# Another order of the same steps for a recurrence followed by a feed-forward block, with two filler matmuls fewer

## The chip, the cores and the metric

The kernel runs on one core of one Trainium2 chip. The metric is the device time of one execution in microseconds (us), given as the median of several executions. A run is called slow when it is more than 1.5% above the fastest of the same kernel; slow runs are left out of ratios. Engines are named as the profile names them: PE (tensor engine), PEld (its weight loads), DVE (vector), ACT (scalar), POOL (GpSimd), SP (the sync engine, which here only issues transfers).

## The reference

Two stages follow each other. The first is a linear recurrence over 768 time steps for 4 batches and 8 heads of 48 channels; the second is a feed-forward block over the resulting 3072 rows.

```python
for t in range(S):
    cur = np.einsum('bhd,bhe->bhde', u[None] * kt, vt)
    y[:, :, t] = np.einsum('bhd,bhde->bhe', rt, state + cur)
    state = wt[:, :, :, None] * state + np.einsum('bhd,bhe->bhde', kt, vt)
...
h = x @ w_in                       # 3072 x 384  @  384 x 2048
g = 0.5 * h * (1.0 + np.tanh(c * (h + 0.044715 * h * h * h)))
return g @ w_out                   # 3072 x 2048 @ 2048 x 384
```

## The kernel before

The work is cut into 12 units of 256 rows (three stretches of time by four batches). For each unit the recurrence is computed in chunks (scores `mt`, masked into `sc`, products `y`, a state `p`), its rows are transposed, and they go through the two matrix products `mm1` (line 626) and `mm2` (line 652). The order of everything is one list of words. A word is a step, its unit and part, a letter for the engine where there is a choice (A, D, P or S), and after `@` the bank of PE's accumulation memory that it takes.

```python
ORDER = """
const.3.D load.w.0.0 const.2.D load_u.A clr.sc.2.P clr.lwl.0.D load.w.0.1 clr.rq.1.P lnL.0.0
... (101 more lines) ...
"""
for word in ORDER.split():
    ... # load ACT's table set if this word needs another one
    step(word)
```

Each engine is given its instructions in the order of the list, and in the traces of both kernels they start in it, by kind of step: in each trace all 607 instructions of ACT, DVE, POOL and SP that I could match to words, and of PE's matmuls 2,278 of 2,280 before and 2,274 of 2,278 after the change; the few others are score products that start up to 0.04 us ahead of the last ones of a state product. So a word that waits holds up what stands behind it on its engine. The steps that the argument touches:

```python
def warm(i, e):                        # i filler matmuls ("dummies"), results never read
    t = bank([P, 512], FP, f"dummy{i}")
    for _ in range(i):
        PE.matmul(t[:, 0:256], warm_src[:, 0:P], warm_src, start=True, stop=True)

def sel(q, e):                         # the diagonal term of a unit, on PE
    ... PE.matmul(st["y", q][c2], diag[...], st["vsc", q][...], ...)

def p(q, e):                           # a unit's addition to the state, on PE
    ... PE.matmul(p2[c2][:, g, :], kt[rows, g, t2, :, :], vt[rows, t2, ds(2 * g, 2), :], **flags)

def mm1(q, i, e):                      # 6 matmuls of 256 columns
    ... PE.matmul(h[:, f, :], w_t, xt[:, :, cb, :], ...)

def ob(q, c2, e): ...                  # copy of a result, on ACT or DVE
def store(q, c2, e):                   # one or two transfers, issued by ACT or by SP
    ... (ACT if e == "A" else SP).dma_start(out=out[ds(row + i, n), cols], in_=t[ds(i, n)])
```

A dummy is a weight load and a matmul in PE's stream of instructions (the trace has 50 of each). The list has 50 of them, all before the first `mm1`. They are there to keep PE busy in the start-up; run u3 below shows what happens to PE's clock without 34 of them.

Of the kernel before, what the change touches and what calls it, by code (L numbers as in the profile page):

```python
# [29 lines left out]
const.3.D load.w.0.0 const.2.D load_u.A clr.sc.2.P clr.lwl.0.D load.w.0.1 clr.rq.1.P lnL.0.0  # L30
clr.sc.0.D const.0 clr.S.0.D clr.kk.2.D clr.lwl.1.P clr.rq.0.P load.w.1 clr.sc.1.P lnL.0.1
warm.16@0 cm.0@0 const.1.P clr.S.1.D lnL.1 ep.0@1 load.k.0 warm.1@2 cx.0@2 clr.kk.1.D
const.4.P ub@3 load.r.0 uc.A cz.0@4 clr.kk.0.D em.0 ez.0 clr.sc.3.D cz.1@5 cx.1@6 ex.0
const.6.A load.r.1 kk.0.0 kk.0.1 load.k.1 rq.0.0 rq.0.1 cm.1@7 ex.1 rq.1.0 warm.2@3 T.0.0@3
ep.1@0 rq.1.1 em.1 rka.0.P warm.3@2 T.0.1@2 load_win.1 load.v.0 warm.4@1 T.1.1@1 Tc.0.0.D
ez.1 clr.lw.2.D load.v.1 kk.1.0 rkb.0.P kk.1.1 Tc.0.1.A load.w.2 Tc.1.1.A load.k.2 al.1
mt.0.1@60 vb.0.A load_win.0 dg.0 rka.1.P mk.0.1.0 load.r.2 al.0 mt.0.0@32 warm.4@7 T.1.0@7
rkb.1.P Tc.1.0.A vb.1.A load.v.2 mk.0.0.0 warm.5@1 p.0@15 mk.0.1.1 mk.0.0.1 warm.4@4
mt.1.0@46 load_win.3 load.w.3 vsc.0 warm.7@3 y.0.0@37 load.k.3 sm.0.0 mk.1.0.0 mt.1.1@02
dg.1 y.0.1 vsc.1 ww.2.P const.5.A warm.4@1 p.1@14 load_win.2 sel.0 mk.1.1.0 a5.0.1 mk.1.0.1  # L40
mk.1.1.1 y.1.0@06 xs.0.0.D sm.1.0 y.1.1 X.0.0@2 clr.rq.2.P xs.0.1.A ln.2 sa.0.1 kw.2.P X.0.1
cum.2@7 Xc.0.A sel.1 a5.1.1 xd.2@1 clr.lw.1.P xs.1.0.A ez.2 xs.1.1.A mm1.0.3@3 sm.0.1
load.w.4 mm1.0.0@2 load.r.3 load.k.4 al.2 ex.2 X.1.0@0 rka.2.P X.1.1 kk.2.0 mm1.0.2@5
mm1.0.1@6 kk.2.1 load_wout.0 rw.2.P Xc.1.D T.2.0@7 mm1.1.2@0 gl.0.2 mm1.0.7@5 gl.0.3
clr.S.3.D rq.2.0 Tc.2.0.A gl.1.2 mm1.1.7@3 sa.1.1 rq.2.1 mm1.1.3@7 gl.0.0 rkb.2.P clr.S.2.D
mm1.0.6@0 clr.lw.0.P gl.0.1 T.2.1@1 sm.1.1 gl.1.3 dg.2 gl.1.7 load_wout.1 mm1.1.6@2 load.r.4
gl.1.6 load.v.4 Tc.2.1.D mm1.1.1@6 gl.0.6 dI.2.1 mm1.0.5@7 mt.2.1@43 dI.2.0 mt.2.0@21 gl.0.7
vb.2.A mk.2.1.0 gl.1.1 mk.2.0.0 mm1.0.4@0 gl.0.4 gl.0.5 load.k.6 mm1.1.0@5 ww.3.P mk.2.0.1
mm1.1.5@4 rka.3.P load.v.3 kw.3.P mk.2.1.1 load.k.5 gl.1.5 mm1.1.4@6 gl.1.0 y.2.0@20 load.w.5
gl.1.4 p.2@17 ww.4.P y.2.1 mm2.0.1.0@3 mm2.1.1.0@4 ln.3 mm2.0.0.0@5 rw.3.P mm2.1.1.1  # L50
mm2.1.1.2 mm2.0.1.1 mm2.0.0.1 mm2.0.0.2 sm.2.0 load.v.5 xs.2.0.D cum.3@6 rkb.3.P mm2.0.1.2
mm2.1.1.3 mm2.1.0.0@1 mm2.0.1.3 mm2.0.0.3 mm2.1.0.1 a5.2.1 xs.2.1.D X.2.0@2 mm2.1.0.2 xd.3@0
mm2.0.0.4 mm2.1.1.4 mm2.0.0.5 mm2.1.1.5 sa.2.1 mm2.1.1.6 mm2.0.0.6 sm.2.1 load.w.6 mm2.1.0.3
mm2.0.1.4 ex.3 mm2.0.1.5 al.3 mm2.1.1.7 ez.3 kk.3.0 mm2.1.0.4 ln.4 rq.3.0 X.2.1 Xc.2.A kw.4.P
kk.3.1 rw.4.P rq.3.1 mm2.1.0.5 load.r.7 mm2.0.1.6 cum.4@7 mm2.0.1.7 xd.4@0 dg.3 ob.1.1.A
load.r.5 ob.0.1.A T.3.1@6 ez.4 mm2.0.0.7 rka.4.P mm2.1.0.6 mm1.2.0@2 Tc.3.1.D ex.4
store.0.1.S ob.0.0.D T.3.0@4 rq.4.0 mm2.1.0.7 mm1.2.1@3 Tc.3.0.D dI.3.0 dI.3.1 al.4 mm1.2.4@6
mm1.2.3@5 gl.2.0 ob.1.0.A gl.2.1 store.0.0.S store.1.1.S gl.2.4 rkb.4.P rq.4.1 kk.4.0
mt.3.1@24 kk.4.1 vb.3.A load.k.7 load.r.6 mt.3.0@10 mk.3.0.0 store.1.0.S mm1.2.6@3 gl.2.3
mm1.2.2@6 mm1.2.5@7 mk.3.0.1 mk.3.1.0 vb.4.A mm2.2.1.0@1 mm2.2.1.1 p.3@50 gl.2.2 ww.5.P  # L60
rka.5.P gl.2.6 kw.6.P y.3.0@26 kw.5.P mk.3.1.1 gl.2.5 y.3.1 p.4@34 sm.3.0 dg.4 mm2.2.1.2 ln.5
sa.3.1 sa.4.0 mm2.2.1.3 mm2.2.0.0@7 a5.3.1 xs.3.0.A mm1.2.7@5 mm2.2.1.4 dI.4.1 sm.3.1 sm.4.0
mm2.2.0.1 mm2.2.0.2 X.3.0@2 mm2.2.1.5 xs.3.1.A sa.4.1 X.3.1 ww.6.P vb.5.P T.4.0@6 mm2.2.0.3
mm2.2.0.4 rw.5.P cum.5@0 mm2.2.1.6 mm2.2.0.5 xd.5@3 gl.2.7 load.w.7 Tc.4.0.D mm2.2.1.7 Xc.3.A
T.4.1@5 al.5 mm1.3.7@2 ex.5 mm2.2.0.6 ez.5 sm.4.1 mm2.2.0.7 rq.5.0 mm1.3.4@6 ln.6 Tc.4.1.D
gl.3.7 rq.5.1 mm1.3.1@4 ob.2.0.D kk.5.0 rkb.5.P mm1.3.0@5 mm1.3.3@3 kk.5.1 mt.4.0@27 ob.2.1.A
dI.4.0 mt.4.1@10 gl.3.1 dg.5 mm1.3.5@4 gl.3.0 mm2.3.0.0@5 gl.3.4 load.w.8 mk.4.1.0 rw.6.P
load.k.8 gl.3.5 mm1.3.6@6 mk.4.0.0 mm1.3.2@1 gl.3.3 mk.4.1.1 mk.4.0.1 dI.5.0 mm2.3.0.1 gl.3.6
ww.7.P cum.6@2 xd.6@7 p.5@43 y.4.0@06 gl.3.2 y.4.1 load.v.6 mm2.3.0.2 mm2.3.0.3 ez.6 sa.5.0
a5.4.1 Td.5.1 kw.7.P mm2.3.0.4 mm2.3.1.0@1 sm.5.0 ln.7 ex.6 store.2.0.S load.w.9 mm2.3.1.1  # L70
ww.8.P kk.6.0 mm2.3.0.5 xs.4.1.A dI.5.1 a5.4.0 sa.5.1 rw.7.P mm2.3.1.2 T.5.0@4 rka.6.P kk.6.1
mm2.3.0.6 cum.7@6 xs.4.0.A X.4.0@0 load.r.8 mm2.3.0.7 rq.6.0 mm2.3.1.3 rq.6.1 X.4.1 mm2.3.1.4
mm2.3.1.5 rka.7.P Tc.5.0.A al.6 sm.5.1 load.w.10 ob.3.0.A rkb.6.P mt.5.1@74 mt.5.0@23
mm2.3.1.6 xd.7@5 mk.5.1.0 mm2.3.1.7 Xc.4.A mk.5.0.0 al.7 mk.5.0.1 ez.7 mm1.4.0@0 vb.6.P ex.7
Td.6.0 ob.3.1.D mk.5.1.1 mm1.4.4@7 ln.8 mm1.4.6@2 gl.4.0 rkb.7.P kk.7.0 mm1.4.1@3 mm1.4.3@1
mm1.4.7@0 kk.7.1 gl.4.6 gl.4.1 gl.4.3 y.5.0@42 rq.7.0 p.6@63 y.5.1 a5.5.1 rq.7.1 kw.8.P dg.6
load.v.7 sa.6.0 sm.6.0 sa.6.1 mm2.4.1.0@5 mm1.4.2@1 mm2.4.1.1 a5.5.0 gl.4.7 mm1.4.5@0 gl.4.2
mm2.4.0.0@6 cum.8@1 dI.6.0 ww.10.P gl.4.4 mm2.4.1.2 xs.5.1.A Td.6.1 mm2.4.0.1 mm2.4.0.2
mt.6.1@72 dI.6.1 xs.5.0.D sm.6.1 gl.4.5 store.2.1.S vb.7.A ln.10 xd.8@3 mt.6.0@40 load.v.8
mk.6.1.0 mm2.4.1.3 mm2.4.1.4 al.8 mm2.4.1.5 mk.6.1.1 mk.6.0.0 rw.8.P Td.7.0 rka.8.P ez.8  # L80
mk.6.0.1 ww.9.P ex.8 mm2.4.1.6 X.5.0@7 mm2.4.1.7 X.5.1 mm2.4.0.3 kk.8.0 mm2.4.0.4 load.k.10
ob.4.1.A Xc.5.A dg.7 rq.8.0 rq.8.1 mm2.4.0.5 kk.8.1 load.k.9 p.7@24 sa.7.0 y.6.0@05 sm.7.0
dI.7.0 y.6.1 Td.7.1 dI.7.1 kw.9.P a5.6.0 mm2.4.0.6 xs.6.0.A mm2.4.0.7 mm1.5.0@7 mm1.5.2@3
mm1.5.5@0 load.r.10 ln.9 a5.6.1 Xd.6.0 gl.5.0 gl.5.5 vb.8.P xs.6.1.D gl.5.2 mm1.5.1@1
ob.4.0.D gl.5.1 rkb.8.P mm1.5.3@2 mm1.5.7@7 gl.5.3 sa.7.1 mm1.5.6@0 mt.7.0@53 gl.5.7
mt.7.1@61 p.8@2 rka.9.P sm.7.1 load.r.9 rw.9.P gl.5.6 load.v.9 mm1.5.4@7 mm2.5.1.0@4 cum.10@0
mk.7.0.0 cum.9@5 mk.7.0.1 gl.5.4 mm2.5.1.1 mm2.5.1.2 mk.7.1.0 xd.10@3 mk.7.1.1 Td.8.1 al.9
mm2.5.0.0@7 mm2.5.0.1 mm2.5.1.3 Xd.6.1 rkb.9.P y.7.0@61 y.7.1 mm2.5.0.2 sa.8.0 store.3.1.S
mm2.5.0.3 ex.10 sm.8.0 store.3.0.S mm2.5.1.4 xd.9@2 ex.9 a5.7.0 mm2.5.0.4 Td.8.0 xs.7.0.A
load.w.11 dg.8 mm2.5.1.5 mm2.5.1.6 rq.10.0 rw.10.P rq.9.0 kw.10.P Xd.7.0 a5.7.1 al.10  # L90
rka.10.P rq.9.1 mm2.5.1.7 vb.9.P dI.8.0 ez.9 rq.10.1 store.4.0.A ez.10 mm2.5.0.5 kk.10.0
mm2.5.0.6 ob.5.1.D ww.11.P load.k.11 mm1.6.0@6 dI.8.1 mm1.6.7@2 mm2.5.0.7 gl.6.0 Td.9.1
kk.9.0 mm1.6.4@3 ob.5.0.A kk.10.1 mm1.6.1@4 gl.6.7 xs.7.1.A mm1.6.2@6 Xd.7.1 kk.9.1 gl.6.1
gl.6.4 mt.8.1@07 mt.8.0@52 dg.9 kw.11.P mk.8.0.0 mk.8.0.1 dI.9.0 load.r.11 gl.6.2 p.9@1
mm1.6.3@4 rkb.10.P mm1.6.6@3 mk.8.1.0 mm2.6.0.0@6 mm2.6.0.1 gl.6.3 mk.8.1.1 Td.9.0
mm2.6.1.0@5 sa.9.0 dI.9.1 ln.11 mm2.6.0.2 rw.11.P mm2.6.1.1 mm2.6.1.2 gl.6.6 mm1.6.5@2
y.8.0@40 gl.6.5 y.8.1 sm.9.0 a5.8.0 mm2.6.0.3 mm2.6.1.3 a5.8.1 xs.8.0.D cum.11@7 mm2.6.0.4
xd.11@1 mm2.6.0.5 mm2.6.0.6 al.11 ez.11 mm2.6.1.4 kk.11.0 mm2.6.0.7 ob.6.0.D mm1.7.0@3 ex.11
mm1.7.3@2 Xd.8.0 xs.8.1.D mm1.7.4@4 kk.11.1 mm1.7.1@6 mm2.6.1.5 gl.7.3 gl.7.0 mm1.7.2@0
gl.7.4 mm2.6.1.6 dg.10 rq.11.0 gl.7.1 rka.11.P mt.9.1@72 mt.9.0@34 mm1.7.7@6 gl.7.2 mm1.7.5@0  # L100
mm2.6.1.7 mk.9.1.0 Td.10.0 mk.9.1.1 mm1.7.6@7 mk.9.0.0 store.4.1.S mm2.7.0.0@2 mk.9.0.1
mm2.7.0.1 load.v.10 gl.7.5 rkb.11.P mm2.7.0.2 y.9.0@30 y.9.1 a5.9.0 mm2.7.1.0@4 a5.9.1
mm2.7.0.3 gl.7.6 mm2.7.1.1 mm2.7.1.2 mm2.7.1.3 mm2.7.0.4 vb.10.P dI.10.0 xs.9.0.A Td.10.1
Xd.8.1 mm2.7.1.4 rq.11.1 mm2.7.0.5 Xd.9.0 gl.7.7 mt.10.1@17 dI.10.1 mt.10.0@36 xs.9.1.D
ob.6.1.D p.10@0 mk.10.0.0 mm2.7.0.6 store.5.1.S load.v.11 mk.10.1.0 mm2.7.1.5 mm2.7.0.7
# [639 lines left out]
```

## Time and profile before

| | |
|---|---|
| time, median | 180.57 us (180.31 to 181.15, 4 executions beside the changed kernel) |
| span of the profiled execution | 178.9 us |
| first `mm1` matmul starts | 23.91 us |
| last PE matmul starts | 175.71 us |
| from there to the end of the span | 3.17 us |
| PE idle after the first `mm1`, summed | 8.04 us by my count below |

The three rows of the middle split the span in a ramp, a middle and a tail, and the rest of this text compares kernels by these three numbers. The sum of idle time is the excess of each PE start-to-start distance over the median distance of the same kind of instruction in this kernel, with shorter distances counted against it. It is good for comparing, not as an absolute: between two kernels with the same PE instructions after the first `mm1`, it differs by just as much as the length of that stretch.

### The profile page before, as it was taken

Reading aid. Unit: us, or ns where it says so; the run is one execution under the profiler, and the core shown is the slowest. Engines: PE = TensorE matmul, PEld = TensorE weight load, DVE = VectorE, ACT = ScalarE, POOL = GpSimd, SP = SyncE. Lnnn points to the kernel's source line nnn. Section 1 sums busy time; section 2 is a strip of 40 time slices with the busy share of each in tenths; the row PEclk is TensorE's granted clock in tenths of the full one; section 3 lists DMA queues with packets and bytes.
Section 4 is the critical chain, followed back from the end, with each engine's and each line's share of the span. In section 5 each row is a group of like instructions: output and inputs, shape, how many; then the busy total and the mean of one; then the engine's idle time right before and its main releaser. Section 6 shows DMA issues by size and latency. Waiting matters only on the chain.

```text
span 178.9 us, 5496 instructions
## 1 busy us (share of the span) xinstructions
PE 172.0 (96%) x2280; PEld 135.7 (76%) x2280; DVE 114.6 (64%) x241; ACT 125.1 (70%) x215; POOL 109.9 (61%) x115
## 2 busy tenths in 40 slices
PE   7889889999999999999999999999999999999993
PEld 5456579966697788688689688687688787868772
DVE  7099979634888998989997998676291182200010
ACT  4595499872699998896988599996254644644831
POOL 7499998619998988998969986991514000000000
PEclk9999999999999999999999999999999999999999
DMA  5999999999999999999997879949297312510244
GB/s 136 261 268 238 255 236 266 219 234 234 270 265 221 317 284 171 276 150 239 177 208 173 174 189 206 154 78 199 54 222 84 89 48 66 117 41 0 44 90 134
DMA packets 74954, 31.68 MB, mean 177 GB/s; under 512 B 69681, under 2 KB 74418, under 8 KB 74930
## 3 DMA queue, kind: packets, MB, share of 16 engines
q1 hardware_dynamic: 71744, 26.91, 71.8%
q0 software_dynamic: 2144, 3.15, 9.9%
q10 hardware_dynamic: 1042, 1.28, 2.5%
q8 instruction: 18, 0.29, 0.7%
q14 instruction: 6, 0.05, 0.1%
HBM read 25.17 MB, written 4.72 MB: 167 GB/s over the span
## 4 chain that ended last, share of the span: by engine, by line
PE 79%; ACT 7%; DMA 6%; SPq 5%; POOL 1%; issue 0%
PE h L626 33%; PE o L652 33%; DMA w<-in_w_dram 6%; SPq L290 5%; PE mt L512 3%; ACT g L634 3%; PE y L534 2%; PE y L584 2%; PE T L433 2%; ACT L713 1%; ACT L711 1%; PE p L550 1%; PE Xp L601 1%; PE z L367 1%; ACT logw L328 1%; PE p L554 1%
## 5 line engine op out<-in xcount | busy, mean ns | idle before, releaser
L652 PE MATMUL o<-w_out_sb,g 128*128 128x384 bf16 (+1 forms) x400 | 73.3, 320 | 0.0
L626 PE MATMUL h<-xT,w_in_sb 128*128 128x256 bf16 x576 | 70.2, 273 | 0.2 <-ACT g L634 0.2
L626 PEld LDWEIGHTS <-w_in_sb 128*128 128x128 bf16 x576 | 62.2, 114 | 3.7
L652 PEld LDWEIGHTS <-g 128*128 128x128 bf16 x400 | 36.4, 98 | 16.5 <-ACT g L634 0.3
L634 ACT ACTIVATE g<-h 128x512 bf16<-128x512 f32 x48 | 32.9, 755 | 22.7 <-PE h L626 22.6
L519 DVE CAST_PREDICATED sc<-mask,mt 128x512 bf16<-128x512 uint16 x48 | 30.3, 684 | 10.5 <-PE mt L512 10.2
L638 ACT ACTIVATE g<-h 128x512 bf16<-128x512 f32 x48 | 26.1, 607 | 4.4 <-PE h L626 4.1
L456 POOL TENSOR_TENSOR rk<-k,u_bc 128x768 f32<-128x768 f32 x12 | 21.8, 1817 | 7.7 <-DMA k<-in_k_dram 5.1
L473 POOL TENSOR_TENSOR sc<-eye,dg 128x512 bf16<-128x512 bf16 x20 | 20.6, 1040 | 4.5 <-DVE dg L467 4.5
L462 POOL TENSOR_TENSOR rk<-rk,r 128x768 f32<-128x768 f32 x12 | 21.8, 1817 | 0.2
L272 DVE COPY ob<-o 128x384 f32<-128x384 f32 (+1 forms) x12 | 6.3, 534 | 21.4 <-PE o L652 21.4
L575 DVE TENSOR_TENSOR s<-p,al 64x192 bf16<-64x192 f32 x40 | 14.1, 353 | 2.5 <-PE p L550 1.7
L593 DVE CAST xs<-y 128x384 bf16<-128x384 f32 x12 | 6.7, 555 | 14.0 <-PE y L584 13.9
L711 ACT ACT_TABLE_LOAD x9 | 11.5, 1283 | 1.4 <-PEq L728 1.3
L567 DVE TENSOR_TENSOR p<-p,s 64x192 f32<-64x192 f32 x32 | 11.7, 365 | 0.8
L713 ACT ACT_TABLE_LOAD x9 | 11.5, 1283 | 0.2
L324 POOL TENSOR_TENSOR ww<-w 128x384 f32<-128x384 f32 x10 | 10.0, 1002 | 2.4 <-DMA w<-in_w_dram 2.4
L467 DVE TENSOR_REDUCE dg<-rk 128x16 f32<-128x768 f32 x12 | 11.4, 946 | 0.1
L485 POOL CAST vb<-v 128x768 bf16<-128x768 f32 x6 | 4.9, 821 | 10.1 <-PE h L626 5.9
L400 POOL TENSOR_TENSOR kw<-k,w 128x384 f32<-128x384 f32 x10 | 10.0, 1001 | 0.3 <-DMA k<-in_k_dram 0.3
L319 PE MATMUL dummy<-warm_src 128*128 128x256 bf16 x50 | 8.6, 315 | 1.5 <-DVE warm_src L259 1.1
L406 POOL TENSOR_TENSOR rw<-r,w 128x384 f32<-128x384 f32 x10 | 10.0, 1000 | 0.0
(94 smaller groups left out, 196.9 us busy)
## 6 DMA issues: line engine op xcount, KB each, us to landing
k<-in_k_dram SPq DMA_DIRECT2D x12, 384.0 KB, 5.9
r<-in_r_dram SPq DMA_DIRECT2D x12, 384.0 KB, 5.8
v<-in_v_dram SPq DMA_DIRECT2D x12, 384.0 KB, 5.7
w<-in_w_dram SPq DMA_DIRECT2D x11, 384.0 KB, 5.5
out_dram<-ob SPq DMA_DIRECT2D x12, 192.0 KB, 3.8
w_in_sb<-in_moe_w_in_dram POOLq DMA_DIRECT2D x4, 384.0 KB, 7.6
w_out_sb<-in_moe_w_out_dram POOLq DMA_DIRECT2D x2, 768.0 KB, 9.4
out_dram<-ob SPq DMA_DIRECT2D x11, 96.0 KB, 2.2
```

The source lines that it names most:

```text
L456: ENG[e].tensor_tensor(out=t, in0=st["k", q].rearrange("p h (t d) -> p h t d", t=2), in1=u_bc[:, :, None, :].broadcast_to([P, H, 2, D]), o ...
L462: ENG[e].tensor_tensor(out=t, in0=t, in1=st["r", q].rearrange("p h (t d) -> p h t d", t=2), op=AL.mult)
L473: POOL.tensor_tensor(out=bass.AP(tensor=o.tensor, offset=o.offset, ap=[list(o.ap[0]), [256, 4], [192, 2], [1, 64]]), in0=eye[:, None, None ...
L519: DVE.copy_predicated(scs[q % NSC][n][:, :, j].rearrange("p a b c i -> p a (b c i)"), mask.rearrange("p a b t -> p (a b t)").bitcast(U16)[ ...
L567: DVE.tensor_tensor(out=p2[rows, :, pc], in0=p2[rows, :, pc], in1=s[rows, :, cols], op=AL.add)
L575: DVE.tensor_tensor(out=s[rows, :, cols], in0=p2[rows, :, pc], in1=st["al", q][rows, :, c2][:, :, None].broadcast_to([64, G, D]), op=AL.mult)
L626: PE.matmul(h[:, f, :], w_t, xt[:, :, cb, :], start=(f + cb == 0), stop=(cb == NCB - 1), skip_group_check=True)
L634: ACT.activation(out=t.rearrange("p f (c i s) -> p (f c) s i", c=2, s=2), in_=h.rearrange("p f (c s i) -> p (f c) s i", c=2, s=2), func=AF ...
L638: ACT.activation(out=t, in_=h, func=AF.Gelu_apprx_tanh)
L652: PE.matmul(st["o", q, c2], st["g", q, i][:, f, ts(m, P)], w_out_sb[i * NWO // 8][:, (2 * i + f) % (NFT // NWO), cols], start=(i + f == 0) ...
L711: ACT.preload_act_table_set(EXP_SET)
L713: ACT.preload_act_table(AF.Gelu_apprx_tanh)
```

## The change

The intent: a search over orders, run again with other assumptions (weight loads hold unit loads up for longer, and the first landings come later), gave another list. Only the list differs: 1,018 words in both, the same computing steps, 48 dummies for 50, 14 table loads on ACT for 18. The core of the diff, ramp and tail:

```diff
-warm.16@0 cm.0@0 const.1.P clr.S.1.D lnL.1 ep.0@1 load.k.0 warm.1@2 cx.0@2 clr.kk.1.D
... (7 lines cut)
-dg.1 y.0.1 vsc.1 ww.2.P const.5.A warm.4@1 p.1@14 load_win.2 sel.0 mk.1.1.0 a5.0.1 mk.1.0.1
... (84 lines cut)
-store.9.0.A mm2.11.0.5 store.9.1.S gl.11.7 mm2.11.2.7 store.10.1.S ob.10.0.A mm2.11.0.6
-ob.11.2.D store.10.0.A mm2.11.0.7 mm2.11.1.2 mm2.11.1.3 mm2.11.1.4 ob.11.0.A store.11.2.S
-store.11.0.A mm2.11.1.5 mm2.11.1.6 mm2.11.1.7 ob.11.1.A store.11.1.A
... (2 lines cut)
+warm.18@0 cm.0@0 lnL.1 clr.sc.3.P warm.2@1 ub@1 ep.0@2 cx.0@3 const.4.A cm.1@4 cx.1@5
... (6 lines cut)
+mk.1.0.0 mk.1.0.1 warm.3@2 y.0.0@24 y.0.1 mt.1.1@71 load.w.2 vsc.0 sm.0.0 warm.2@5 p.1@53
+mk.1.1.0 ww.2.P dg.1 warm.6@6 sel.0 a5.0.1 mk.1.1.1 xs.0.0.A y.1.0@67 X.0.0@2 y.1.1 xs.0.1.A
+X.0.1 vsc.1 load.k.2 load_win.2 sa.0.1 ln.2 Xc.0.A load_wout.0 sm.1.0 cum.2@1 rka.2.P sel.1
... (83 lines cut)
+mm2.11.0.6 mm2.11.0.7 mm2.11.2.6 store.9.0.A ob.10.0.D store.9.1.A mm2.11.1.1 mm2.11.2.7
+ob.11.0.A mm2.11.1.2 mm2.11.1.3 ob.10.1.D ob.11.2.D mm2.11.1.4 mm2.11.1.5 mm2.11.1.6
+store.10.1.S store.10.0.S mm2.11.1.7 store.11.0.A store.11.2.S ob.11.1.A store.11.1.A
```

## The prediction

> **What bounds the kernel now.** I read the page first: engine shares, the 40 slices, the chain that ended last.
>
> ```profile
> PE 172.0 (96%) x2280; PEld 135.7 (76%) x2280; DVE 114.6 (64%) x241; ACT 125.1 (70%) x215; POOL 109.9 (61%) x115
> PE   7889889999999999999999999999999999999993
> DMA  5999999999999999999997879949297312510244
> PE 79%; ACT 7%; DMA 6%; SPq 5%; POOL 1%; issue 0%
> ```
>
> The tensor engine is busy in every slice after the first six or so, and 79% of the chain is its own work. The rest of the chain is a start-up (DMA, SPq, POOL) and one piece on ACT. So I split the 178.9 us span in three with the chain in order of time.
>
> ```profile
> 10.78 10.51 DMA w<-in_w_dram
> 21.36 1.01 POOL ww L324
> 22.39 0.53 ACT logw L328
> 22.96 0.32 PE z L367
> ...
> 24.07 1.31 PE h L626 x12
> ...
> 110.28 0.75 ACT g L634
> 111.05 1.28 ACT L711
> 112.35 0.53 ACT logw L328
> 112.89 1.28 ACT L713
> ...
> 121.81 1.47 PE h L626 x12
> ...
> 170.40 5.57 PE o L652 x48
> 175.99 0.33 ACT ob L270
> ```
>
> The reader sees: (1) a ramp until about 23.9, where the first matmul of the feed-forward part (line 626) can start; it ends with the decay load of unit 2, landing at 21.3 after 10.5 us in flight, its product on POOL, its Ln and the copy of unit 0's transposed rows on ACT; (2) about 152 us, 23.9 to 175.95, in which PE runs almost back to back; (3) a tail of 2.9 us: last copy, store, landing.
>
> How much idleness is left in (2)? I took durations from the chain: 12 matmuls of line 626 in 1.31 us, 4 of line 652 in 0.65, 32 score matmuls in 0.57, 8 transposes in 0.45, and so on. Summed in the order of the list, PE has 165.6 us of work, 15.7 of it before the first line-626 matmul, so 149.9 after. Against 152 that leaves about 2.1 us, of which part is error of my rounding; the offset between summed work and the trace's clock grows steadily (8.2 us at unit 0, 9.3 at unit 7) and by about 0.6 across the ACT piece at 110 to 122. That piece is 11.5 us long in the chain, but PE is fed through most of it:
>
> ```profile
> 109.00:122.00 13.00, 12.82 (x191) 10.18 (x182) 8.89 (x17) 12.61 (x18) 11.06 (x9) 1.00 0.83 146
> ```
>
> (columns: length, then busy PE, weight loads, DVE, ACT, POOL, clock, DMA share, GB/s). ACT is full, PE lacks 0.2 us of busy time.
>
> [...] the chain shows 1.31/12 and 0.65/4[...]; here 8 transposes of 128 columns take 0.45[...]. So I take these spacings as fixed. [...] the 576 of line 626 show 273 ns each but follow at 109, which is why I count starts. [...] The trace shows 1283 ns, and the next ACT instruction 1.3 us after the load's start (111.05 to 112.35), so I count 1.28[...]. [...] with both queues loaded, w of unit 2 took 10.5 us against a median of 5.5 for such loads.
>
> **The change, part by part.** Only the list of steps differs, 1,018 words in both. The computing steps are the same.
>
> Dummies: 50 to 48. Their 0.11 to 0.21 us each lie inside waits of the ramp: worth 0.
>
> PE: one transposed pair swaps places (units 4 and 5 lose a PE transpose, 5 and 6 gain one): 0. Work after the first line-626 matmul, summed alike: 165.4 - 15.5 = 149.9, unchanged. So the change can act only through the ramp, idleness, and the tail.
>
> Ramp: SP issues the same sequence of loads up to w of unit 4 and beyond, apart from the two halves of w of unit 0, so w of unit 2 should land within some tenths of 21.3. What moves:
> - u's copy to u_bc now stands behind an eye constant of two ACT instructions (0.54 us), so POOL's first product starts at about 9.0 instead of 8.49, and the first three w_in loads go out about 0.5 us later.
> - On ACT and DVE the exponentials of unit 0 end about 0.5 later (ez.1 and a DVE clear of 0.48 come ahead): the first mask copy ends its group of four at about 17.6, before 17.0.
> - On POOL the second vsc (1.49 us) now stands behind ww of unit 2. Before: vsc, vsc, ww from 18.25 to 22.36. After: vsc 18.8 to 20.3, ww when w lands, about 21.2 to 22.2, then vsc to 23.7. PE needs it for sel.1, which stands ahead of the first line-626 matmul: 0.4 for sel, 0.17 for the state term, so 23.7 + 0.1 + 0.6 = 24.3 to 24.4. If w lands 0.4 earlier because w_in starts 0.5 later, 23.9.
> Sum for the ramp: +0.4 (0 to +0.7).
>
> Weights: the fourth w_in load goes out at about 23.7 (22.3 before) and by its measured 7.6 us lands at 31.3. Its first user comes after ten line-626 groups of 0.656, a transpose of X 0.34 and one of keys 0.45: 24.3 + 7.35 = 31.65. It just fits; before there were over 2 us. The second w_out load stands behind five POOL products (1.82+1.0+1.82+1.0+1.04), so it goes out at about 32 (29.7 before), lands at 41.4 by the 9.4 us of the page, and is needed at about 42.6. It fits by 1 us. In return k and r of unit 3, which in the trace took up to 15.6 us, meet one weight load less just when they are due: this was a wait of 5.1 us on POOL, off PE's path.
>
> ACT: 18 table loads become 14: -4 x 1.28 = -5.1 us. More copies of y (16 for 12, +2.0), outputs (15 for 13, +1.0), one constant (+0.55), five more store DMAs issued (14 for 9, at 0.4 to 0.55: +2.3); two copies of Xp fewer (-1.6), one vb fewer (-0.9). Sum -1.8 us of ACT. Two of the four fall around unit 5, two around units 9 to 11, where ACT was full: I give -0.4 us of PE idleness.
>
> Tail: the last piece is the same, but the stores of unit 10 stand at the very end on SP: four issues and then one of unit 11, in place of unit 10 being already on its way. +0.2.
>
> Sum: +0.4 - 0.4 + 0.2 = +0.2, and a little for waits that a list made for other landings will meet in one of twelve units: +0.1. 180.6 + 0.3 = 180.9.
>
> **The rivals.** First: a landing misses. Then PE, which takes its instructions in order, stops for the whole miss: the fourth w_in or second w_out load late by 1 to 2 us gives 182 to 183. For it: both fit by no more than 1 us in my count, and DMA is at nine tenths until slice 20. Against: the list was made for longer hold-ups, and w_in's spread in the trace is only 7.2 to 8.2.
> Second: ACT relief is worth more. If all of the 2.1 us of idleness in the middle belongs to ACT's piece and similar ones, the change could bring 179.0 to 179.5. For it: two table loads fewer just where the chain leaves PE. Against: PE lacked only 0.2 us of busy time there, and DVE stays at its count.
> Third: the ramp. If the recurrent part of units 0 and 1 is really ready earlier, w of unit 2 still holds the first matmul by its landing plus 2.55 us (ww, Ln, copy of X), so the gain is hidden: 180.5.
> Fourth: a buffer chain. POOL is given 14 us of work in about 10 us of PE's time around unit 6; if it falls behind, the diagonal it writes holds the y of a unit: 182.
>
> **Range and chances.** A floor comes from the count: a start at 23.9, 149.9 of work, 2.9 of tail and the 1.7 between span and time give 178.4, so 2% faster (177.0) is out of reach: 0.01. Slower by 2% is 184.2, over 3 us of waits: two misses together, 0.05. Within 2%: 0.94. Eight times in ten I expect 179.3 to 182.6, wider above because every miss adds and the floor is near.
>
> **What would show it.** Right: the first line-626 matmul at 24.0 to 24.7, with POOL's second vsc ending last before it; PE's line again at nine tenths throughout; ACT's table loads 7 and 7; the ACT piece at 110 to 122 gone from the chain; DMA's or POOL's share of the chain no larger than 8%. Wrong: PE idle on a weight load of w_in or w_out (first rival), the span below 177.5 (second), the first line-626 matmul before 23.5 or after 25.5, or y waiting for POOL's sc writes (fourth).

The 1283 ns that "the trace shows" there are one table load on ACT (the page of the kernel before: 18 of them, 1,283 ns each in the mean).

## More of the kernel before

The prediction shows the shares and the chain. Two more views matter later. First PE's timeline in the ramp (columns: start, length, engine, line, operation, names, shapes, count, and in brackets the idle time ahead and what ended it):

```profile
19.26 0.60 PE L319 MATMUL dummy<-warm_src 128*128 128x256 bf16 x4 [0.47 <-DVE dg L467]
19.91 0.51 PE L550 MATMUL p<-vb,kk 64*128 64x96 bf16 x16
20.27 0.49 PE L500 MATMUL y<-vsc,diag 64*128 64x384 bf16 x4
...
22.96 0.32 PE L367 MATMUL z<-logw,incl 128*128 128x384 bf16 x1 [0.91 <-ACT logw L328]
```

The dummies of line 319 stand behind a wait, and the diagonal term of unit 0 (line 500) starts at 20.27. Before the first `mm1`, PE waits another 0.91 us for the Ln of unit 2 on ACT, so work ahead of that wait has some slack. Second, the tail, transfers and copies only:

```profile
174.74 0.34 SPq L668 DMA_DIRECT2D out_dram<-ob  x1
175.00 0.49 ACT L270 ACTIVATE ob<-o 128x384 f32<-128x384 f32 x1 [1.47 <-PE o L652]
175.52 0.34 ACTq L668 DMA_DIRECT2D out_dram<-ob  x1
175.99 0.33 ACT L270 ACTIVATE ob<-o 128x192 f32<-128x192 f32 x1 [0.50 <-PE o L652]
176.35 0.34 ACTq L668 DMA_DIRECT2D out_dram<-ob  x1
```

Only three stores are issued after 174.7, and the last lands at 177.98.

## The result, and the profile after

The changed kernel took 182.62 us in the median (182.03 to 183.09, 4 executions, all at a clock of 0.997 or more) against 180.57 of the kernel before. The ratio is 1.0108, with a 95% interval of 1.0069 to 1.0146. Here and below a ratio is the mean time of one kernel's fast runs over that of the other's of the same rounds, so it is not quite the ratio of the medians. In class this is "within 2%", as predicted, and the sign is right, but the loss is 2.05 us and not 0.3, and 182.62 lies 0.02 outside the range (179.3 to 182.6). The profiled execution of the changed kernel is the slowest of the four, 183.09 us.

The page of the changed kernel, in the parts that answer to those of before:

```profile
PE 172.5 (95%) x2278; PEld 135.1 (75%) x2278; DVE 112.1 (62%) x234; ACT 121.4 (67%) x216; POOL 111.9 (62%) x117
...
PE 81%; DMA 7%; ACT 5%; SPq 3%; issue 1%; DVE 1%; DVEq 0%
```

PE's work is the same and ACT has 3.7 us less, so the shares of busy time say that the new order is no worse. The three numbers say otherwise:

| profiled execution | first `mm1` | idle after it | last PE start to end | span |
|---|---|---|---|---|
| before | 23.91 | 8.04 | 3.17 | 178.88 |
| after | 24.65 | 8.70 | 3.99 | 181.09 |
| difference | +0.74 | +0.66 | +0.82 | +2.21 |

The three add up to the difference of the spans (+2.22 against +2.21); by the way the idle time is counted they must, so this is no check. Each place can be seen. In the ramp, the chain in order of time (start, length, what):

```profile
19.82 0.26 PE p L550 x3
20.07 0.48 issue
20.55 0.45 PE p L550 x13
21.01 0.76 PE dummy L319 x6
21.77 0.43 PE y L500 x4
...
24.81 1.31 PE h L626 x12
```

PE stops in the middle of a state product for 0.48 us with "issue", which means that the profile shows nothing it waited for. Then come six dummies, on the chain with 0.76 us, and only then the diagonal term (line 500). (The chain counts a group from where the one before it ended; by the instruction's own record that matmul starts at 21.70, 1.43 us later than before, and the first one of line 626 at 24.65.) Of these 1.43 us only 0.74 reach `mm1`: the wait of 0.91 us for the Ln of unit 2 is gone, and the work between is 0.22 us longer. In the middle, the one large wait of PE (us in total, times, longest), and its place in the chain:

```profile
PE h L626 <- DMA xT<-xs: 0.7, 1, 0.7
```

```profile
126.48 5.28 DMA xT<-xs
131.75 0.14 issue
131.89 4.75 PE h L626 x42
```

The second half of unit 8's rows is transposed by a transfer that SP issues at 126.48, behind two transposes of another unit, and `mm1` of unit 8 waits for it. In the tail:

```profile
175.22 3.03 SPq L668 DMA_DIRECT2D out_dram<-ob  x5
175.90 0.49 ACT L270 ACTIVATE ob<-o 128x384 f32<-128x384 f32 x1 [3.82 <-PE o L652]
...
177.38 0.33 ACT L270 ACTIVATE ob<-o 128x192 f32<-128x192 f32 x1 [0.99 <-PE o L652]
177.75 0.36 ACTq L668 DMA_DIRECT2D out_dram<-ob  x1
```

Both stores of unit 10, four transfers, and one of unit 11 are issued by SP in one row of five from 175.22. The fifth is issued only at 177.71 and lands at 180.13, the last landing of all; ACT's last, issued at 177.75, lands at 179.87. Before, nothing landed after 177.98. ACT's last store also travels longer beside SP's row: 2.12 us from issue to landing, 1.63 before.

### The profile page after: what moved, and what is told of

Its sections match the earlier page's. It is cut to its first block, busy times and chain, and to the rows that moved or that the text cites. A ratio compares the mean times of both kernels' runs of the same rounds, so it can differ in the third digit from the quotient of the medians.

```text
span 181.1 us, 5496 instructions
## 1 busy us (share of the span) xinstructions
PE 172.5 (95%) x2278; PEld 135.1 (75%) x2278; DVE 112.1 (62%) x234; ACT 121.4 (67%) x216; POOL 111.9 (62%) x117
## 4 chain that ended last, share of the span: by engine, by line
PE 81%; DMA 7%; ACT 5%; SPq 3%; issue 1%; DVE 1%; DVEq 0%
PE o L652 32%; PE h L626 32%; DMA r<-in_r_dram 4%; PE y L534 3%; DMA xT<-xs 3%; PE mt L512 3%; PE T L433 2%; PE y L584 2%; PE p L550 2%; ACT T L440 2%; SPq L290 1%; SPq L449 1%; PE Xp L601 1%; ACT g L634 1%; PE z L367 1%
## 5 line engine op out<-in xcount | busy, mean ns | idle before, releaser
L272 DVE COPY ob<-o 128x384 f32<-128x384 f32 (+1 forms) x10 | 5.2, 534 | 24.2 <-PE o L652 13.4
L591 ACT ACTIVATE xs<-y 128x384 bf16<-128x384 f32 x16 | 7.5, 488 | 10.9 <-PE y L584 6.2
L424 DVE TENSOR_TENSOR rq<-r,x 128x384 bf16<-128x384 f32 x12 | 6.6, 550 | 8.8 <-DMA r<-in_r_dram 6.7
L593 DVE CAST xs<-y 128x384 bf16<-128x384 f32 x8 | 4.5, 556 | 12.2 <-PE y L584 12.1
L270 ACT ACTIVATE ob<-o 128x384 f32<-128x384 f32 (+1 forms) x15 | 7.0, 481 | 7.0 <-PE o L652 7.0
```

## The experiments

The theory: three separate losses, the dummies ahead of the diagonal term, the stores on SP, and an order in the middle with no margin for late landings. The rivals: the second `vsc` on POOL sets the ramp (the prediction's own mechanism), or one of the three causes the others. Twelve runs were made, on three chips (r, s and u below); a ratio is always to the kernel before on the same chip, from fast runs alone, while a median is over all executions (r1, r3, s2 and u4 have one slow execution each). The third column gives how many of the executions had a mean granted clock below 0.992; one stretch of 3.41 us at half the clock, as measured in s2 and s3 below, makes about 0.99 of a mean over 179 us (an estimate: 1 - 0.5 x 3.41 / 179).

| kernel | time, median | low clock | ratio [95%] | first `mm1` | idle | tail |
|---|---|---|---|---|---|---|
| r1 changed, again | 183.30 | 2 of 6 | 1.0133 [1.0099, 1.0168] | 24.54 | 9.70 | 3.97 |
| r2 without six dummies | 182.00 | 2 of 6 | 1.0089 [1.0054, 1.0123] | 23.91 | 8.03 | 3.85 |
| r3 before's ramp, then changed | 182.38 | 0 of 6 | 1.0118 [1.0076, 1.0159] | 23.85 | 8.69 | 3.81 |
| r4 changed ramp, then before's | 183.03 | 0 of 4 | 1.0140 [1.0116, 1.0165] | 24.47 | 9.45 | 3.18 |
| s1 changed, unit 10 ends earlier | 182.86 | 3 of 6 | 1.0086 [1.0040, 1.0133] | 24.33 | 7.85 | 3.97 |
| s2 changed, two transfers earlier | 182.81 | 3 of 6 | 1.0054 [1.0000, 1.0107] | 26.16 | 7.80 | 4.02 |
| s3 edits of r2, s1 and s2 together | 182.61 | 2 of 6 | 1.0073 [1.0024, 1.0122] | 24.57 | 8.21 | 4.58 |
| s4 before, copy of rows first | 181.43 | 1 of 6 | 1.0002 [0.9969, 1.0034] | 22.92 | 9.05 | 3.17 |
| u1 changed, `store.10.0` on ACT | 182.08 | 0 of 6 | 1.0046 [0.9998, 1.0093] | 25.14 | 8.12 | 3.17 |
| u2 changed, dummies laid otherwise | 183.87 | 4 of 6 | 1.0161 [1.0109, 1.0213] | 24.98 | 7.85 | 4.09 |
| u3 before, 16 dummies | 183.01 | 6 of 6 | 1.0099 [1.0052, 1.0146] | 24.30 | 9.99 | 3.17 |
| u4 before, copies of rows first | 180.74 | 0 of 6 | 0.9973 [0.9925, 1.0021] | 22.65 | 8.74 | 3.18 |

The kernel before took 180.52, 181.45 and 181.16 us on the three chips. The last three columns come from one profiled execution each. On the last chip the kernel before had three of eleven executions at 183.0 to 183.5 with the clock at 0.999 or 1.0; what made them long isn't seen, since only one execution is profiled. In r2, r3 and r4 the list is three lines shorter, so line numbers there are three less.

**r1: the changed kernel again.** No edit.

> The changed kernel once more, as the control of this batch. Every theory: 182.5 us, 1.0 to 1.1% over the kernel before; the profile shows the first line-626 matmul at 24.6 to 24.8, a wait of PE on an xT transpose of 0.5 to 0.9 near 131, and 3.6 to 3.8 us from the last matmul to the end. If one of the three is missing in this second profile, it was chance of one execution.

The loss is there again, with 24.54 for the ramp and 3.97 for the tail, close to the first profile. The middle is not the same: the wait for the transposed rows of unit 8 is gone, and four others, of 0.16 to 0.41 us as the profile counts them, stand between 98 and 113. The first goes back to one landing; that the other three do is my reading. SP reached the load of w of unit 10 at 91.47 rather than 89.38, because a pair of transposes ahead of it took 4.67 rather than 2.56 us; on POOL the product that needs this load then waited:

```profile
L400 POOL TENSOR_TENSOR kw<-k,w 128x384 f32<-128x384 f32 x3 | 3.0, 1000 | 3.0 <-DVE s L575 2.3 <-DMA k<-in_k_dram 0.7
```

(columns after the bars: busy us and mean ns, idle time ahead and what ended it). The label names DVE for 2.3 us; the last landing before the instruction was w, so by the landing times it was the load. The lesson is that the middle of this order has little slack, and where it loses differs between executions.

**r2: the six dummies ahead of the diagonal term taken out.**

```diff
-mk.1.1.0 ww.2.P dg.1 warm.6@6 sel.0 a5.0.1
+mk.1.1.0 ww.2.P dg.1 sel.0 a5.0.1
```

> The changed kernel without the group of six dummy matmuls that PE runs between the state product of unit 1 and the diagonal term of unit 0. Theory 'dummies on the path': the diagonal term starts when POOL's vsc ends (20.8) instead of 21.7, and all that hangs on it moves up: first line-626 matmul 0.5 to 0.8 earlier, time 181.8 to 182.0. Rival 'dummies fill a wait': the first line-626 matmul stays at 24.65, held by ww, Ln and the copy of X, and the time stays at 182.5.

```profile
19.47 0.26 PE L547 MATMUL p<-vb,kk 64*128 64x96 bf16 x3
20.70 0.45 PE L547 MATMUL p<-vb,kk 64*128 64x96 bf16 x13 [0.97 <-issue]
20.97 0.51 PE L497 MATMUL y<-vsc,diag 64*128 64x384 bf16 x4
```

The first `mm1` starts at 23.91, exactly as in the kernel before, although the second `vsc` still stands behind `ww` of unit 2 on POOL (21.51 to 23.00). So the six dummies were the ramp's loss in this profile, and `vsc` was not. The ratio went from 1.0133 to 1.0089, 0.8 us on the same chip, though the intervals overlap. Two of six executions had a low clock, as in r1, so in this small sample taking these dummies out didn't make that worse. The stop of 0.97 us inside `p` remained; more on it below.

**r3 and r4: the two halves exchanged.** The words ahead of the first `mm1` come from one list, the others from the other list; where a bank was still taken, another was given (5 banks in r3, 14 in r4).

```diff
 r3:  words of before up to the first mm1, then the remaining words in the changed order
 r4:  words of the changed kernel up to the first mm1, then the remaining words in the order before
```

> All steps that stand ahead of the first line-626 matmul in the kernel before, in the order of before, then the rest in the changed kernel's order (a few PSUM banks renamed where the two halves clash). Theory 'ramp, middle and tail each lost some 0.7': first line-626 matmul at 23.9, time 181.8. Rival 'the ramp is hidden by a later wait': first line-626 matmul at 23.9 but time 182.4 or more. Rival 'the ramp is all': 180.6.

> The opposite: the changed kernel's steps ahead of its first line-626 matmul, then the rest in the order of before. Theory 'ramp, middle and tail each lost some 0.7': 181.3 with the first line-626 matmul at 24.65. Rival 'the ramp is all': 182.5. Rival 'hidden': 180.6.

Each half brings what belongs to it: r3 starts `mm1` at 23.85 and has a tail of 3.81, r4 starts at 24.47 and has one of 3.18. But both times are as bad as the whole change, because each has new waits of its own just behind the seam: 0.68 and 0.28 us at 34 to 35 in r3, 0.52 at 27.3 and 0.84 at 37.7 in r4. Two lists that were each tuned as a whole can't be split by joining halves. This is a weak experiment, and I put no sum on it.

**s1: unit 10's last products, copies and stores pulled ahead.**

```diff
-mm2.10.1.5 mm1.11.5@6 mm2.11.0.0@1 ...
+mm2.10.1.5 mm2.10.0.6 mm2.10.1.6 mm2.10.0.7 mm2.10.1.7 ob.10.0.D ob.10.1.D store.10.1.S store.10.0.S mm1.11.5@6 mm2.11.0.0@1 ...
```

> The changed kernel with the last four matmul pairs of unit 10 pulled ahead of those of unit 11, and its copies and stores with them. Theory 'the late stores of unit 10 lengthen the tail by some 0.7': from the start of the last matmul to the end 3.2 us as in the kernel before (3.9 now), time lower by 0.6 to 0.8, 182.0 or so. Rival 'the tail is the last copy, store and landing alone': no change, 182.6 to 183.

A miss for this way of mending the tail, which stayed at 3.97. The chain shows why:

```profile
172.04 3.92 DMA out_dram<-ob
...
176.11 0.50 ACT ob L270
...
177.02 0.33 ACT ob L270
```

The stores of units 9 and 10 now go out together from 170.6 to 173.4, and one took 3.92 us. In the tail of this profile stores landed after 1.6 to 4.0 us with a median of 2.3, against 1.6 to 2.6 with 2.1 in the kernel before and 2.1 to 3.6 with 2.3 in the changed one; that they slow each other is my reading. ACT's copy for unit 11 uses the buffer of unit 9 again and waits for that store, so the last copy starts 1.09 us after the last matmul, where it was 0.28. One wait took the place of the other.

**s2: two of SP's transfers earlier.** The load of w of unit 10 goes ahead of a store, and unit 8's second transpose ahead of the load of v of unit 10.

```diff
-store.2.0.S ... load.w.10
+load.w.10 store.2.0.S ...
-load.v.10 ... Xd.8.1
+Xd.8.1 load.v.10 ...
```

> The changed kernel with two entries of SP's queue moved up: w of unit 10 ahead of a store and two transposes, and the second xT transpose of unit 8 ahead of a load and a transpose. Theory 'the middle is lost where SP's queue is late': no PE gap over 0.3 us between 95 and 132, the profiled executions lose 0.8 (first) and 1.7 (second) there now, so 0.5 to 1.5 less on average, 181.5 to 182.3, and a narrower spread than 181.9 to 184.0. Rival 'the waits only move on to the next transfer': the same gaps elsewhere, time unchanged.

After the ramp the profile lists no wait of PE (it lists those above 0.15 us), and the sum is 7.80. That fits the theory but doesn't show it: r2, s1, u1 and u2, which have the changed order in the middle without this edit, list no wait there either and come to 7.85 to 8.12. The late landings of the first profile and of r1 are met in some executions only, and two profiles of six can't tell whether s2 removes them. But the ramp of this profile ended at 26.16. The profile of stretches of 3.41 us (length, busy PE, weight loads, DVE, ACT, POOL, clock, DMA share, GB/s) shows what happened to it:

```profile
18.04:21.45 3.41, 2.29 (x70) 1.55 (x69) 3.35 (x8) 0.74 (x5) 3.24 (x4) 1.00 1.19 236
21.45:24.86 3.41, 3.41 (x49) 1.85 (x46) 2.06 (x6) 1.45 (x3) 3.22 (x4) 0.50 1.21 251
```

For one stretch PE had half its clock. The stretch before it is the one in which PE was busy for only 2.29 of 3.41 us. The edit is at 89 us and later, so it isn't the cause; this is the ramp of the changed kernel, in an execution where the clock dropped. The three executions of s2 that kept the clock took 181.83 us in the mean, about 0.4 us over the kernel before on this chip; three are few, but they suggest that much of what s2 still loses is the dropped clock.

**s3: the edits of r2, s1 and s2 together.**

> The changed kernel without the six dummies, with the moved tail and the two moved entries of SP's queue. If the loss is the sum of ramp 0.75, middle 0.7 to 1.7 and tail 0.7: 180.2 to 180.8, the time of the kernel before. If something else is at work: 181.3 or more.

182.61, no better than its parts. The profiled execution had a half-clock stretch at 7.24 (PE busy 2.11 us of the 3.41 ahead of it), and the tail was worst of all at 4.58, since s1's edit was a bad one. It settles nothing about the sum of the parts.

**s4 and u4: the other way round, the kernel before with the copy of unit 0's rows ahead of unit 2's Ln.** The prediction had noted that the ramp ends with Ln and then this copy on ACT.

```diff
 s4:
-xs.0.1.A ln.2 sa.0.1 ... cum.2@7 Xc.0.A sel.1 a5.1.1 xd.2@1 ... ez.2 xs.1.1.A mm1.0.3@3
+xs.0.1.A sa.0.1 ... Xc.0.A ln.2 sel.1 a5.1.1 ... xs.1.1.A mm1.0.3@3 cum.2@7 xd.2@1 ez.2
 u4, besides:
-mm1.0.3@3 cum.2@7 xd.2@1 ez.2 sm.0.1 ... X.1.1 kk.2.0 ... Xc.1.D T.2.0@7 mm1.1.2@0
+mm1.0.3@3 sm.0.1 cum.2@7 xd.2@1 ez.2 ... X.1.1 Xc.1.D kk.2.0 ... mm1.1.2@0 T.2.0@7
```

> The kernel before with unit 0's copy of X ahead of unit 2's Ln on ACT, and the first line-626 group ahead of unit 2's cumulative product on PE, so that the feed-forward part no longer waits for unit 2's load of w. Theory 'the ramp sets the time, as PE is full after it': first line-626 matmul at 23.0 in place of 23.9, time 179.6 to 180.0, better than both kernels. Rival 'the gelu copies on ACT, or a later wait, take it back': first matmul at 23.0, gaps of PE before 35, time 180.3 to 180.8.

> The kernel before with the copies that the first matmuls of w_in need put ahead of the next unit's work on ScalarE and VectorE for both halves, and the matmul that frees the bank moved with them. Theory (the 1 us that the earlier copy gained was given back where a bank was freed behind the next unit's state on VectorE, and the two further moves mend this): first matmul of w_in at 22.9, no gap over 0.5 us up to 30 us, ratio 0.996 to 0.999. Rival (what is put back, the next unit's chain, comes late in its turn and takes it): ratio 1.000 to 1.003 with a new gap at 26 to 36 us.

In s4 the first `mm1` started at 22.92, 1.0 us earlier, and the time was the same (1.0002): the third group then waited for a bank that `sm.0.1` frees, which stood behind unit 2's subtraction on DVE.

```profile
25.46 0.71 PE L626 MATMUL h<-xT,w_in_sb 128*128 128x256 bf16 x5 [0.46 <-DVE s L575]
```

In u4 that wait is gone, a smaller one has come, and the last PE matmul starts at 175.27, 0.43 us earlier than before:

```profile
27.44 0.82 PE L626 MATMUL h<-xT,w_in_sb 128*128 128x256 bf16 x6 [0.30 <-ACT g L638]
```

So of 1.26 us won in the ramp 0.43 reached the end. The ratio 0.9973 has an interval that holds 1.0: this may be a slightly better kernel than both, but the runs don't show it.

**u1: one word of the change undone in the tail.**

```diff
-mm2.11.1.1 mm2.11.2.7 ob.11.0.A
+mm2.11.1.1 mm2.11.2.7 store.10.0.A ob.11.0.A
-store.10.1.S store.10.0.S mm2.11.1.7
+store.10.1.S mm2.11.1.7
```

> The changed kernel with one part of the change undone: the store of the first half of unit 10 goes back from SyncE's queue to ScalarE's, ahead of the second copy of unit 11. Theory (the tail's 0.8 us are the stores that queue on SyncE at the end): the time from the last PE instruction's start to the end of the span falls from 3.99 us to 3.2 to 3.7 and the time by 0.3 to 0.7 us, to a ratio of about 1.007. Rival (the store's issue holds ScalarE's last copies up, or the copies wait for their buffer): the tail stays at 3.8 or more and the ratio at 1.010 to 1.013.

```profile
174.67 1.13 ACTq L668 DMA_DIRECT2D out_dram<-ob  x2
175.13 1.93 SPq L668 DMA_DIRECT2D out_dram<-ob  x3
175.93 0.49 ACT L270 ACTIVATE ob<-o 128x384 f32<-128x384 f32 x1 [3.93 <-DMA out_dram<-ob]
```

The tail fell from 3.99 to 3.17, the value of the kernel before. SP's row is now three transfers long, its last is issued at 176.70 and lands at 178.85, and ACT's last copy is no later. So the tail's loss is shown to be this one word. The ratio is 1.0046, against 1.0108 and 1.0133 for the whole change on other chips; the whole change didn't run on this one, where the kernel before had its long executions, so the ratios alone prove little. What remains of the profiled span is in the ramp, which in this profile ended second latest of all, and without any half-clock stretch:

```profile
19.54 0.26 PE L550 MATMUL p<-vb,kk 64*128 64x96 bf16 x3
21.04 0.45 PE L550 MATMUL p<-vb,kk 64*128 64x96 bf16 x13 [1.25 <-issue]
21.43 0.83 PE L319 MATMUL dummy<-warm_src 128*128 128x256 bf16 x6
22.19 0.50 PE L500 MATMUL y<-vsc,diag 64*128 64x384 bf16 x4
```

The stop inside `p` was 1.25 us here, 0.48 in the first profile of the same ramp.

**u2: the changed kernel's dummies laid where PE seemed to wait.**

```diff
-const.4.A cm.1@4 ... warm.4@6 p.0@60 ... warm.2@5 p.1@53 ... dg.1 warm.6@6 sel.0
+const.4.A warm.4@4 cm.1@4 ... warm.4@6 warm.5@6 p.0@60 ... warm.2@5 warm.6@5 p.1@53 ... dg.1 sel.0
```

> The changed kernel with its dummies laid otherwise: the six ahead of the diagonal term of the first unit are gone, and fifteen are added at three places where PE waits for ScalarE or VectorE in the ramp (57 in all). Theory (the change's dummies are in the way at one place and lacking at others, so that the clock drops for a window in some executions): the first matmul of w_in at 23.9 to 24.2 instead of 24.5 to 24.65, no execution with a granted clock under 0.992 out of six, median 181.3 to 181.9, ratio 1.004 to 1.008. Rival (the low windows are chance and have nothing to do with dummies): two of six executions low again, and 182 or more.

A miss on both counts: the first `mm1` came at 24.98, and four of six executions had a low clock, with more dummies than in any other kernel.

```profile
18.85 0.36 PE L512 MATMUL mt<-T,T 48*64 48x128 bf16 x12
20.18 0.25 PE L512 MATMUL mt<-T,T 48*64 48x128 bf16 x4 [0.97 <-issue]
20.36 1.26 PE L319 MATMUL dummy<-warm_src 128*128 128x256 bf16 x8
21.69 0.52 PE L550 MATMUL p<-vb,kk 64*128 64x96 bf16 x16
22.04 0.49 PE L500 MATMUL y<-vsc,diag 64*128 64x384 bf16 x4
```

The stop has moved. It is no longer in `p` but in the scores ahead of it, and eight dummies that were to fill it now stand behind it, in the way.

**u3: the kernel before with its first 16 dummies only.**

```diff
-warm.1@2 ... warm.2@3 ... warm.3@2 ... warm.4@1 ... warm.4@7 ... warm.5@1 ... warm.4@4 ... warm.7@3 ... warm.4@1
```

> The kernel before with only its first 16 dummies (34 taken away), nothing else changed. Theory (dummies keep the clock up in the ramp): a third or more of the executions, or all, have a half-clock window of some 3.4 us in the ramp, a mean clock of 0.98 to 0.991, and are 1 to 2 us longer; ratio 1.003 to 1.012. Rival (the later dummies are idle padding that does nothing): ratio 0.998 to 1.002 and all clocks at 0.995 or more.

```profile
PEclk9996558999999999999999999999999999999999
```

```profile
11.20:14.62 3.42, 2.16 (x48) 1.55 (x49) 3.42 (x8) 2.79 (x4) 3.40 (x3) 1.00 1.27 251
...
14.60:28.20 13.60, 12.04 (x177) 8.34 (x177) 10.69 (x22) 7.23 (x17) 12.92 (x14) 0.50 1.19 247
```

All six executions had a low clock, 0.962 to 0.981, and took 1.0099 times as long. In the profile PE had half its clock from 14.62 to 28.27, after a stretch in which it was busy for 2.16 of 3.42 us. So the dummies do carry the clock in this ramp, and 34 of them are worth some 1.8 us (183.01 against 181.16). At half the clock PE was busy for 2.89, 3.01 and 2.80 us in the next three stretches, and the clock stayed down; it came back after a stretch that was busy throughout (3.42 of 3.42 us). The three drops in the ramps of the 14 profiles came after stretches with PE busy for 2.29 (s2), 2.11 (s3) and 2.16 us (u3) of 3.41. After those with 2.43 us or more the full clock never dropped, but one of u1 with 2.10 us (from 19.09) wasn't followed by a drop either, so no clean threshold can be read from this.

### What the stop called "issue" is

Number everything that the trace records of PE's stream from 0: weight loads, matmuls, and the four to six semaphore and drain instructions among them. In every kernel but one the stop ends with number 449, whatever stands there. (By weight loads and matmuls alone it is 443 with the changed ramp and 445 with the ramp of before, so what stays fixed is the place in the stream of instructions.) The traces also hold the packets of a queue that the page lists as carrying instructions (packets, MB, share of the transfer engines' time):

```profile
q8 instruction: 18, 0.29, 0.7%
```

Its packets are 16,384 bytes each. For the first of them in the span and for number 449:

| kernel | packet starts | landed | 449 starts | after landing | after number 448 | what 449 is |
|---|---|---|---|---|---|---|
| before | 16.70 | 17.72 | 19.26 | 1.54 | 0.54 | a dummy |
| after | 17.98 | 19.22 | 20.55 | 1.33 | 0.68 | in `p.1` |
| r1 | 17.82 | 19.06 | 20.44 | 1.38 | 0.73 | in `p.1` |
| r2 | 18.02 | 19.23 | 20.70 | 1.47 | 1.18 | in `p.1` |
| s2 | 18.65 | 19.61 | 20.84 | 1.23 | 1.21 | in `p.1` |
| u1 | 18.61 | 19.75 | 21.04 | 1.29 | 1.45 | in `p.1` |
| u2 | 17.76 | 18.93 | 20.18 | 1.25 | 1.19 | in `mt.1.1` |
| u3 | 16.68 | 17.74 | 20.65 | 2.91 | none | in `y.1.0` |

The other six profiles fall in the same ranges (1.23 to 1.54 after the landing). In u3, with 34 dummies fewer, PE comes to number 449 much later and passes it without a stop. The 18 packets of the kernel before are on average 246 recorded instructions of PE apart (4,176 over 17). When the first of them starts, PE is at number 301 to 405 in the 14 profiles, so 44 to 148 ahead of number 449. After the ramp PE needs longer for 246 instructions in the mean (about 9.6 us in the kernel before, against 6.20 from number 203 to 449), though its fastest 246 there take 5.1 us; and in the lists of waits of the changed kernel, s2 and u1 a wait of PE for "issue" stands once only, this one.

So the reading is: PE ran out of instructions in the ramp, where many short matmuls follow each other, and the next ones were still on their way through transfer engines that the loads fill (DMA stands at nine tenths in slices 2 to 20 of the page of the kernel before). This is inferred and not shown. It rests on 14 traces, one number that stays fixed while the work around it moves, and one kernel that reaches it late and doesn't stop. What it doesn't rest on is an experiment made for it. That the travel is long because the loads fill the transfer engines is not shown either, and that the profiler itself makes the stop is a rival that no run excludes, though u3, profiled the same way, has none. In the kernel before, the profile gives the wait at number 449 to DVE, and whether DVE or the packet ended it I can't tell.

## Why the prediction was right or wrong

The class was right and so was the sign. Of the sum, four terms were tested.

**Ramp: +0.4 predicted, +0.74 measured, and the mechanism was wrong.** The prediction put the loss on "the second vsc (1.49 us)", ending at 23.7 and holding `sel.1`. It ended at 23.35, and the second diagonal term started at 24.04 behind other PE work. r2 kept that order on POOL and started `mm1` at 23.91, as before. A number near the right one came out of the wrong step.

**"Dummies: ... worth 0": wrong twice.** This is the step that failed most. First, six of them were on the path with 0.76 us, because PE came so late, with the stop of 0.48 us in `p.1`, that the diagonal term's data had long been ready (`vsc` of unit 0 ended at 20.80, the term started at 21.70). Without the stop the term would have started at about 21.22 (an estimate, 21.70 - 0.48), so some 0.42 us of the dummies would have been on the path all the same. Nor was there a later wait to hide them, as the one of 0.91 us in the kernel before might have. r2 showed their worth. Second, dummies and clock: u3 shows that dummies as such hold the clock, and by count the changed ramp holds it less well. Over all runs 16 of 50 executions with that ramp (r2 and u2 included) had a clock below 0.992, against 2 of 51 with the ramp of before and all its dummies (33 of the kernel before on the three chips, and those of r3, s4 and u4). It is the same on each of the three chips: 4 of 16 against 0 of 17, 8 of 18 against 2 of 17, 4 of 12 against 0 of 17. In r2 the two low executions took 183.2 us in the mean, the other four 181.7; in u2 four took 184.2 and two 183.0. That the number of dummies, 48 or 50, isn't what matters is shown by u2, which had 57. Where they stand, and where PE stops, decides how full the worst stretch is; that last step is argued from the profiles and not shown by a run.

**ACT: -0.4 predicted, at most some 0.2 seen.** The table loads fell to 7 and 7 and ACT's busy time by 3.7 us; the prediction's sum without the issues of stores, which the profile doesn't count as busy, is 4.05. But idle time after the first `mm1` was 8.70 and 9.70 in the two profiles of the changed kernel against 8.04 before. The relief was real, but there was next to nothing to win: in the kernel before the profile lists one wait of PE for ACT after the first `mm1`, 0.2 us. In the changed kernel PE waited for a landing behind a full SP queue (first profile), and in r1 first for a product of POOL that another late landing held up (two short waits there, of 0.19 and 0.16 us, were ended by ACT). In the four profiles with the changed middle and no such wait (r2, s1, u1, u2) the idle time is 7.85 to 8.12, so ACT's relief brought 0.2 us at most. The first rival of the prediction ("a landing misses") was right in kind, but it named the weights, which did not miss; it was the transposed rows of unit 8 and w of unit 10.

**Tail: +0.2 predicted, +0.82 measured.** The mechanism was right: stores of unit 10 at the very end on SP. Its size was wrong. I counted the issues and not that the last of them must still travel: five issues in a row push the last landing from 177.98 to 180.13, while the last matmul moved only by 1.4. Even without SP's fifth store the last landing would have been ACT's at 179.87, since that store itself took 0.49 us longer to land than the last one of the kernel before. u1 took one word back and got the whole 0.82.

The remaining rivals: the ramp wasn't hidden, and POOL's chain did not fall behind in the first profile; in r1 it did, behind the late load of w of unit 10, and the first of PE's four waits there is for a copy that POOL makes for unit 8. Three of the signs that the prediction named as showing it right came true all the same: `mm1` started at 24.65, the table loads were 7 and 7, and DMA's share of the chain was 7%. Two of them are counts, and the first was reached on another path. The sign that tests the mechanism, `vsc` ending last ahead of `mm1`, did not come true, and a piece on ACT stayed in the chain, from 118.1 to 122.6.

Open: whether the edits of r2, s2 and u1 together give back the whole time, as s3 ran with the bad edit of s1 and no run has these three; why PE reaches the instruction 246 places ahead of number 449 at 14.54 in the changed kernel and at 13.06 before (the sum of small moves that the prediction lists is 0.5); what makes single executions of the kernel before 2.5 us long at full clock; and whether the packet's travel or the dummies should be mended first in this ramp.

## What to carry to other kernels

A filler instruction isn't free because PE "waits anyway": ask what it waits for, and whether that is over by the time PE gets there, since PE takes it in order and the stream behind it moves (six of them stood on the chain with 0.76 us here). Where a profile shows a stop with no reason, number the engine's instructions in several kernels: a stop that stays at one number while the work around it changes (449 here) points to the stream of instructions and not to the data. In a tail, follow each store to its landing and spread the issues over the queues (one store moved from SP's to ACT's took the tail from 3.99 to 3.17 us in u1); the last landing ends the kernel (180.13 in the changed one), not the last product (started at 177.10).
